# Chunk-selecting attention with a softplus MLP on one core: transposes by DMA, halved first preparation, a new load order

## The chip, the cores and the metric

The kernel runs on one core of one Trainium2 chip. The metric is the device time of one execution in microseconds (us), as a median over several executions. Names used below: PE is TensorE (PEld its weight loads), DVE is VectorE, ACT is ScalarE, POOL is GpSimd, SP is SyncE, which here only issues DMAs.

## The reference

```python
# q, k, v: (4 batches, 8 heads, 768, 64); moe_w_in: (512, 2048); moe_w_out: (2048, 512); all float32
k_min, k_max = min and max of k over each chunk of 32 keys          # 24 chunks
ub = sum_d(max(q * k_min, q * k_max))                               # upper bound for each query and chunk
top_chunks = the 6 chunks of highest ub (only chunks up to the query's own)
attn = softmax(q @ k.T / 8, over the keys of those chunks, causal)
x = (attn @ v) with the heads side by side                          # (3072, 512)
h = x @ w_in
g = max(h, 0) + log1p(exp(-abs(h)))                                 # softplus
out = g @ w_out                                                     # (3072, 512)
```

## The kernel before

The work goes in 12 blocks of 256 queries. A block has four parts: *preparation* (turn k and q so that the head dimension lies on the partitions, chunk minima and maxima `kx`, bounds `ub`, the mask), *scores* (`s_ps`, `exp` into `pt`), *AV* (`o_ps`, normalised into `o_sb`, turned into `x`), and the *MLP* (`hp`, softplus, `y`). Preparation, attention and MLP of different blocks are interleaved by slots: a slot is one `yield` of the score loop. Block 3i has 8 slots, block 3i+1 has 16, block 3i+2 has 24.

Every transpose is a TensorE matmul with the identity, followed by a copy out of PSUM, the memory that matmuls write to:

```python
def prep_block(n):                                     # cut
    kT = ps_t.tile([128, NP, QB], BF16, name="kT", tag="t")
    for t in range(NT):
        for p in range(NP):
            nc.tensor.transpose(kT[:, p, t * 128:(t + 1) * 128], k_sb[:, t, 2 * p:2 * p + 2, :], ident)
    nc.scalar.copy(kt, kT)
    nc.vector.tensor_reduce(kx[:, :, 0], kT4, axis=AX.X, op=ALU.max)    # kT4 is a view of kt
    nc.vector.tensor_reduce(kx[:, :, 1], kT4, axis=AX.X, op=ALU.min)
    ...
    yield
    # then qT in the same way, the bounds, and mT, the transposed mask
def ot_step(n, p, o_sb):
    oT = ps_t.tile([128, QB], BF16, name="oT", tag="t")
    for u in range(NT):
        nc.tensor.transpose(oT[:, u * 128:(u + 1) * 128], o_sb[:, u], ident)
    nc.vector.tensor_copy(X[n][:, p], oT)
```

Blocks 0 to 2 are loaded as float32 by SP (half of block 0 by ACT's queue) and cast by ACT; later blocks and the weights are loaded by POOL with a cast in the DMA. The order is: blocks 0, 1, 2, then w_in, then w_out.

The order of the instructions on an engine is either that of the source ("manual") or that of the compiler's list scheduler. POOL and SP are manual throughout. PE, ACT and DVE are manual in block 0 alone:

```python
ctx.enter_context(tc.manual_schedule(engines={ET.Pool, ET.SP}))
...
with tc.manual_schedule(engines={ET.Activation, ET.DVE, ET.PE}):
    ...
    run_block(0, 0.0)
... # cut: block 2's loads
run_block(1, 0.8)
for n in range(2, NB):
    run_block(n, 1.0 if n > 2 else 0.8)
```

The softmax here doesn't subtract the row's maximum and nothing guards it: scores larger than these inputs give would overflow.

## Time and profile before

| | before |
|---|---|
| median of the first three runs | 316.74 us (316.65 to 318.0) |
| profiled span | 314.1 us |
| PE, ACT, DVE busy | 86%, 71%, 56% |
| first `exp` of block 2 | 55.7 us |
| from there to the end | 258.4 us |

The last two rows are read from ACT's timeline, by counting its `exp` instructions (8, 16, 24 for a block). They split the span into a start, in which PE starves, and a later stage.

The first lines of the page of the kernel before. The strings of digits cut the span into 40 slices; a digit is the busy share of a slice in tenths, PEclk is the clock granted to TensorE in tenths.

```profile
span 314.1 us, 6878 instructions
...
PE 270.5 (86%) x2748; PEld 198.6 (63%) x2784; DVE 174.4 (56%) x550; ACT 224.2 (71%) x379; POOL 99.0 (32%) x172
...
PE   1335879989899799899999799899999999999983
...
PEclk9999959999999999999999999999999999999999
DMA  9999899993933906904913905907900000001101
```

PE is thin for five slices (40 us), then near full. Next, groups of the same kernel: line, engine, operation, tiles, shapes, count, then busy time in us and mean ns of one, then the idle time of the engine just before them and what ended it.

```profile
L305 DVE COPY x<-oT 128x256 bf16<-128x256 bf16 x48 | 13.9, 289 | 25.1 <-PE oT L304 24.8
...
L304 PE MATMUL oT<-ident,o_sb 128*128 128x128 bf16 x96 | 13.7, 225 | 4.3 <-DVE o_sb L293 4.3
...
L236 PE MATMUL mT<-ident,mraw_114 128*64 128x128 bf16 x48 | 4.7, 253 | 3.4 <-DVE mraw_114 L230 3.2
```

These are the round trips that the change wants to remove: PE waits for DVE, turns, and DVE copies back.

### The profile page before, as it was taken

The page shows a single profiled execution, that of the slowest core. Times are in us where ns is not written, and L with a number is a line of the kernel's source. Part 1 is how long each engine was busy: PE and PEld are TensorE (multiplying, and loading weights), DVE is VectorE, ACT ScalarE, POOL GpSimd, SP SyncE. Part 2 cuts the span into 40 slices and gives each one's busy share as a digit, 9 for nine tenths or more (in the row PEclk, how much of TensorE's full clock was granted, in tenths as well). Part 3 has the DMA queues.
Part 4 walks back from the last instruction along what each step waited for, and adds up shares of the span by engine and source line. Part 5 has one row for each costly group of instructions (what it writes and reads, how often), then busy time and mean ns, then how long its engine had stood idle before and what let it go on. Part 6 is the DMA issues. An engine that isn't in the chain of part 4 may idle for free.

```text
span 314.1 us, 6878 instructions
## 1 busy us (share of the span) xinstructions
PE 270.5 (86%) x2748; PEld 198.6 (63%) x2784; DVE 174.4 (56%) x550; ACT 224.2 (71%) x379; POOL 99.0 (32%) x172
## 2 busy tenths in 40 slices
PE   1335879989899799899999799899999999999983
PEld 0223657667658667677658577677568777776651
DVE  5818582592965964935946946836748732112100
ACT  4578789968837858788628868888539769983550
POOL 4024375622723613514624414424421211111000
PEclk9999959999999999999999999999999999999999
DMA  9999899993933906904913905907900000001101
GB/s 165 200 216 216 147 158 189 92 71 45 80 73 52 83 11 60 101 2 57 90 59 53 83 35 33 102 3 76 94 33 35 3 33 35 2 33 35 67 17 52
DMA packets 82208, 23.51 MB, mean 75 GB/s; under 512 B 75520, under 2 KB 78080, under 8 KB 82176
## 3 DMA queue, kind: packets, MB, share of 16 engines
q0 software_dynamic: 59424, 11.28, 43.9%
q1 hardware_dynamic: 19632, 11.01, 14.3%
q10 hardware_dynamic: 3120, 0.79, 1.4%
q8 instruction: 21, 0.34, 0.4%
q14 instruction: 11, 0.09, 0.1%
HBM read 27.26 MB, written 6.29 MB: 107 GB/s over the span
## 4 chain that ended last, share of the span: by engine, by line
PE 57%; DVE 26%; ACT 12%; issue 2%; DMA 1%; ACTq 0%; DVEq 0%
PE y L335 21%; PE hp L322 17%; PE o_ps L285 5%; PE s_ps L263 4%; DVE kx L181 4%; ACT kt L179 4%; DVE kx L182 4%; PE s_ps L265 3%; PE mT L236 3%; ACT pt L267 2%; DVE qneg L204 2%; ACT e_sb L324 2%; DVE qpos L203 2%; DVE qt L200 2%; DMA xf<-in_k_dram 1%
## 5 line engine op out<-in xcount | busy, mean ns | idle before, releaser
L267 ACT ACTIVATE pt<-s_ps 128x512 bf16<-128x512 f32 (+1 forms) x192 | 103.9, 556 | 36.7 <-PE s_ps L265 29.9
L322 PE MATMUL hp<-x,w_in_sb 128*128 128x256 bf16 x768 | 103.5, 273 | 3.2 <-ACT e_sb L324 1.8
L271 POOL TENSOR_SCALAR_AFFINE_SELECT pt<-pt 128x256 bf16<-128x256 bf16 x96 | 40.9, 426 | 185.5 <-ACT pt L267 185.1
L335 PE MATMUL y<-w_out_sb,g 128*128 128x512 bf16 x348 | 90.7, 379 | 3.6 <-DVE y_sb L340 1.7
L322 PEld LDWEIGHTS <-w_in_sb 128*128 128x128 bf16 x768 | 71.4, 98 | 12.9 <-issue 4.1
L324 ACT ACTIVATE e_sb<-hp 128x512 f32<-128x512 f32 x96 | 58.4, 611 | 27.7 <-PE hp L322 27.4
L335 PEld LDWEIGHTS <-g 128*128 128x128 bf16 x384 | 34.2, 97 | 28.6 <-issue 2.8
L326 ACT ACTIVATE g<-e_sb 128x1024 bf16<-128x1024 f32 x48 | 51.8, 1078 | 0.3
L285 PEld LDWEIGHTS <-pt 128*128 128x128 bf16 x672 | 32.9, 99 | 11.1 <-issue 4.3
L340 DVE COPY y_sb<-y 128x512 f32<-128x512 f32 x24 | 16.5, 687 | 39.7 <-PE y L335 39.5
L291 DVE RECIPROCAL rec<-o_ps 128x4 f32<-128x4 f32 x48 | 8.5, 177 | 38.1 <-PE o_ps L285 37.9
L305 DVE COPY x<-oT 128x256 bf16<-128x256 bf16 x48 | 13.9, 289 | 25.1 <-PE oT L304 24.8
L285 PE MATMUL o_ps<-v_106,pt 128*128 128x65 bf16 x336 | 20.7, 199 | 2.2 <-DVE o_sb L293 1.9
L181 DVE TENSOR_REDUCE kx<-kt 128x32 bf16<-128x1024 bf16 x12 | 14.6, 1219 | 13.0 <-ACT kt L179 13.0
L293 DVE TENSOR_TENSOR o_sb<-o_ps,rec 128x256 bf16<-128x256 f32 x48 | 20.2, 422 | 1.3
L285 PE MATMUL o_ps<-v_107,pt 128*128 128x65 bf16 x336 | 18.4, 193 | 1.7 <-DVE o_sb L293 1.5
L304 PE MATMUL oT<-ident,o_sb 128*128 128x128 bf16 x96 | 13.7, 225 | 4.3 <-DVE o_sb L293 4.3
L114 POOL DMA_DIRECT2D k_sb<-in_k_dram x18 | 16.1, 892 | 0.8 <-issue 0.5
L114 POOL DMA_DIRECT2D q_sb<-in_q_dram x18 | 16.2, 902 | 0.4 <-issue 0.3
L175 PE MATMUL kT<-ident,k_sb 128*128 128x128 bf16 x96 | 8.8, 241 | 8.1 <-ACT k_sb L103 7.6
L263 PE MATMUL s_ps<-qt,kb_110 128*128 128x256 bf16 x48 | 14.0, 293 | 1.6 <-ACT pt L267 0.9
L263 PE MATMUL s_ps<-qa,ka_108 96*128 96x256 bf16 x48 | 14.2, 296 | 0.8 <-DVE qa L241 0.8
(111 smaller groups left out, 365.2 us busy)
## 6 DMA issues: line engine op xcount, KB each, us to landing
out_dram<-y_sb SPq DMA_DIRECT2D x24, 256.0 KB, 2.0
k_sb<-in_k_dram POOLq DMA_DIRECT2D x18, 128.0 KB, 3.8
q_sb<-in_q_dram POOLq DMA_DIRECT2D x18, 128.0 KB, 4.3
w_in_sb<-in_moe_w_in_dram POOLq DMA_DIRECT2D x8, 256.0 KB, 6.9
w_out_sb<-in_moe_w_out_dram POOLq DMA_DIRECT2D x4, 512.0 KB, 9.5
v_107<-in_v_dram POOLq DMA_DIRECT2D x12, 128.0 KB, 5.3
xf<-in_k_dram SPq DMA_DIRECT2D x5, 256.0 KB, 5.1
xf<-in_q_dram SPq DMA_DIRECT2D x5, 256.0 KB, 5.8
```

The costliest lines, as they stand in the source:

```text
L114: nc.gpsimd.dma_start(out=xb[:, t], in_=rows(nm, n, t))
L181: nc.vector.tensor_reduce(kx[:, :, 0], kT4, axis=AX.X, op=ALU.max)
L263: nc.tensor.matmul(s_ps[:, 0:QB], kk[0:nr, p, j * 128:(j + 1) * 128], qq[0:nr, p, :], start=True, stop=True)
L267: nc.scalar.activation(pt[:, h, j:j + 2].rearrange("k j c -> k (j c)")[:, 0:w], s_ps[:, 0:w], ACT.Exp, scale=scale)
L271: nc.gpsimd.affine_select(out=diag, in_=diag, compare_op=ALU.is_ge, fill=0.0, base=0, channel_multiplier=-1, pattern=[[0, 2], [1, 128]])
L285: nc.tensor.matmul(o_ps[:, u, h], pt[:, h, j, c0:c0 + 128], V[b % 2][:, j, 2 * p + h, :], start=(j == 0), stop=(j == t0 + u))
L293: nc.vector.tensor_tensor(o_sb, o_ps[:, :, :, 0:D], rec.to_broadcast([128, NT, 2, D]), op=ALU.mult)
L322: nc.tensor.matmul(hp[:, fi], w_in_sb[:, dt, ft * 128:(ft + 1) * 128], X[n][:, dt], start=(dt == 0), stop=(dt == KDM - 1))
L324: nc.scalar.activation(e_sb[:, f2 * 2:f2 * 2 + 2], hp, ACT.Exp)
L326: nc.scalar.activation(g[:, f4 * 4:(f4 + 1) * 4], e_sb, ACT.Ln, bias=1.0)
L335: nc.tensor.matmul(y, g[:, f, u * 128:(u + 1) * 128], w_out_sb[:, f, :], start=(f == 0), stop=(f == KFF - 1))
L340: nc.vector.tensor_copy(y_sb, y)
```

## The change

From block 2 on, k, q and the mask are transposed by DMA, and in every block the output; these DMAs (*turns*) are issued on the SP queue. The chunk extremes `kx` of these blocks are now called `kxf`. The first two blocks are prepared by halves of the head pairs. The loads come as blocks 0 and 1, w_in, w_out, block 2. PSUM is dealt out anew, and some pools have more buffers. The core of the diff, with cuts:

```diff
-    pt_pool = ctx.enter_context(tc.tile_pool(name="pt", bufs=3))
+    pt_pool = ctx.enter_context(tc.tile_pool(name="pt", bufs=5))
-    ps_o = ctx.enter_context(tc.tile_pool(name="ps_o", bufs=1, space=PS))
-    ps_t = ctx.enter_context(tc.tile_pool(name="ps_t", bufs=2, space=PS))
+    ps_o = ctx.enter_context(tc.tile_pool(name="ps_o", bufs=2, space=PS))
+    ps_t = ctx.enter_context(tc.tile_pool(name="ps_t", bufs=1, space=PS))
...
+    def turn_dma(nm, n, pool):
+        x_sb = loaded.pop((nm, n))
+        xt = pool.tile([128, NT, NP, 128], BF16, name=nm + "t")
+        nc.sync.dma_start_transpose(out=xt.rearrange("d t p s -> d (t p) s"),
+                                    in_=x_sb.rearrange("s t h d -> s (t h d)"))
+        turned[nm, n] = xt
...
     def prep_block(n):                                 # from block 2 on
-        (kT by TensorE, copy by ACT)
+        kt = turned.pop(("k", n))
+        kx = prep.tile([128, 2, NT, NP, CH // 8], BF16, name="kxf")
         for t in range(NT):
+            kc = kt[:, t].rearrange("d p (c e) -> d p c e", e=CH)
+            nc.vector.tensor_reduce(kx[:, 0, t], kc, axis=AX.X, op=ALU.max)
+            nc.vector.tensor_reduce(kx[:, 1, t], kc, axis=AX.X, op=ALU.min)
+            yield
...
+        nc.sync.dma_start_transpose(out=mt.rearrange("c t g s -> c (t g) s"),
+                                    in_=mraw.rearrange("s t p h c -> s (t p h c)"))
...
     def ot_step(n, g, o_sb):                           # two head pairs at a time
+        nc.sync.dma_start_transpose(
+            out=X[n][:, g].rearrange("d u p s -> d (u p) s"),
+            in_=o_sb.rearrange("s u p h d -> s (u p h d)"))
+        if g == 1:
+            ready[n] = clock[0] + 4                    # hp waits 4 slots more
...
+        base = PER * (n - 1) - PER // 2 + 2            # kxf stands in slot base; 17 for block 2
+        at(base - (4 if n > 2 else 1), turns)          # the turn of k
+        at(base - (3 if n > 2 else 1), turns)          # the turn of q
...
+        at(1, hold(xfs["q", 1][0:1, 1, 7, 0:1]))       # POOL waits for block 1's q
+        loads.append(load_w_in())
+        loads.append(load_cast("v", 1))
+        loads.append(load_w_out())
+        block_loads(2)
```

## The prediction

> **What bounds the kernel now.** Span 314.1 us; engine shares: PE 86%, ACT 71%, DVE 56%. Until about 60 us PE starves (slice row 1, 3, 3, 5, 8 tenths at first), waiting for loads and the preparation chains of blocks 0 to 2; w_in's last piece is issued at 36.2 us and lands about 7 us later; w_out's last is issued at 43.4 and first used at 58.6. After that PE is the limit. Start-to-start distances of matmuls in dense stretches of the timeline: 109 ns for 256 columns, 215 for 512, about 30 for the 65-column AV matmuls, 56 for a 128x128 transpose. All matmuls at these distances are about 249 us of PE work: hp 84, y 83, scores 36, AV 20, transposes 21, bounds 5. By 60 us only 22 us is done; the other 227 take 254 us, so about 27 us of the later stage is waiting. The groups table places some: oT 4.3 us for o_sb, mT 5.1, AV 3.9; the distances before oT and mT matmuls from 60 to 300 us add to 18 us for 8.6 us of work. The chain of waits has DVE 26% and ACT 12%, mostly preparation.
>
> **Removed.** PE loses 344 of 384 transposes (the instruction order shows 688 fewer PE rows, matmul plus weight load): 344 x 56 ns = 19 us, about 17 of it after 60 us. DVE loses 48 oT copies (13.9 us) and 9 qT copies (6.1); ACT loses kt and qt copies of 1.0 us and casts. Round trips for oT and mT vanish; two AV banks, five pt and x buffers loosen the rest.
>
> **Added.** Five transposing DMAs a block on the SP queue, 0.9 MB. None is in this trace. The Trainium skill ("DMA: Bandwidth & Descriptors", section "Latency and other measured facts") states 261 GB/s effective for one kind of transposing DMA; with the 2.0 us that a store takes here from issue to landing, 256 KB would take an estimated 3 us. The schedule gives them 3 to 5 slots of about 1.2 us: hidden, with small stalls.
>
> **Startup.** Blocks 0 and 1 are prepared faster (first scores near 15 us instead of 17; block 1 near 30 instead of 35), and w_in lands 10 us earlier. But block 2's k and q come after w_out, at an estimated 46 to 50 us by the read rates of the trace (about 210 GB/s for float loads, 340 to 400 for the casting weight loads); then transposes, preparation and mask follow. Block 2's scores start near 60 us, as before.
>
> **Sum.** From block 2: 213 us of PE work instead of 227; waiting 27 -> about 17 us, as h-only stretches stay ACT-bound. 60 + 213 + 17 = 290, perhaps 2 less from startup: span 288, time **290 us**, 8-in-10 range **277 to 303**. Chances: faster 0.89, same 0.06, slower 0.05.
>
> **What would show it.** About 2,400 PE matmuls; ACT total about 215 us; transposing DMAs landing in 3 to 5 us; few waits of DVE for kt and qt; w_in landed by 33 us; block 2's scores near 60 us.
>
> **What would make it wrong.** Transposing DMAs of 8 us or more, or queued on SP behind waiting ones: kx and hp would then wait in each block (20 us or more too slow). Block 2's loads landing at 40 us instead of 48: 8 us faster. ACT becoming the limit.

## The result, and the profile after

The changed kernel takes **338.19 us** (336.81 to 338.91, 4 runs) against 317.24 (316.65 to 318.0, 4 runs) for the kernel before: 1.065 times as long, 95% interval 1.0607 to 1.0701. Ratios here are the mean time of one kernel's fast runs over that of the other's fast runs of the same rounds, so they are not quite the ratio of the medians quoted. The prediction was 290 us and faster; the kernel is slower by over 2%.

The same lines of the page of the changed kernel:

```profile
span 337.0 us, 6388 instructions
...
PE 261.4 (78%) x2411; PEld 185.2 (55%) x2440; DVE 168.5 (50%) x615; ACT 197.2 (59%) x350; POOL 115.7 (34%) x191
...
PE   1234579428978879589899699299898799999994
...
PEclk9999999856997999969999979789999799999999
DMA  9929999996995992946966949937946211011101
```

The transposes are gone from PE (2,411 matmuls), and PE is busy for 9 us less, but the span is 23 us longer. PE has a hole near 60 to 80 us and dips all through the later stage, and most dips come with a lower granted clock. The first `exp` of block 2 is at 79.7 us instead of 55.7; from there to the end it is 257.3 us instead of 258.4. So the start lost 24 us, and the later stage gained 1 us in place of the gain of about 28 us that the prediction counted on (258.4 to 213 + 17 = 230).

Who waited for whom in the changed kernel (in us: total, times, longest); the waits for transposing DMAs are new:

```profile
DVE kxf L289 <- DMA kt<-k_sb: 30.1, 9, 7.8
...
PE y L415 <- DVE y_sb L420: 17.2, 7, 6.0
...
PE hp L402 <- DMA x<-o_sb: 11.1, 3, 8.1
...
DVE qa L279 <- DMA mt<-mraw_115: 8.3, 5, 2.7
DVE qa L279 <- DMA mt<-mraw_114: 7.7, 4, 3.3
```

The wait of `y` has a small counterpart in the kernel before:

```profile
PE y L335 <- DVE y_sb L340: 1.7, 3, 0.8
```

The median time from issue to landing of the transposing DMAs:

```profile
x<-o_sb SPq DMA_TRANSPOSE x24, 3.2
...
kt<-k_sb SPq DMA_TRANSPOSE x10, 4.7
qt<-q_sb SPq DMA_TRANSPOSE x10, 5.1
mt<-mraw_114 SPq DMA_TRANSPOSE x5, 2.5
```

That is what the prediction expected in the middle (3 to 5 us). One place of the later stage shows how it hurts all the same. First DVE's timeline around the preparation of block 9 (start, duration, engine, line, operation, in brackets the idle time before it):

```profile
203.77 0.42 DVE L373 TENSOR_TENSOR o_sb<-o_ps,rec 128x256 bf16<-128x256 f32 x1
212.00 0.69 DVE L289 TENSOR_REDUCE kxf<-kt 128x16 bf16<-128x512 bf16 x1 [7.81 <-DMA kt<-k_sb]
...
216.85 0.68 DVE L420 COPY y_sb<-y 128x512 f32<-128x512 f32 x1
```

The SP queue at the same time:

```profile
204.22 1.19 SPq L381 DMA_TRANSPOSE x<-o_sb  x1
205.51 1.25 SPq L166 DMA_TRANSPOSE kt<-k_sb  x1
206.93 1.53 SPq L166 DMA_TRANSPOSE qt<-q_sb  x1
```

And PE:

```profile
217.58 1.86 PE L415 MATMUL y<-w_out_sb,g 128*128 128x512 bf16 x4 [6.02 <-DVE y_sb L420]
```

DVE stands at `kxf` from 204.2 us, 1.3 us *before* the DMA that `kxf` needs is even issued. The k that it turns had been loaded by 186.6 us. The copy `y_sb`, which has nothing to do with block 9, stands behind `kxf`; PE cannot start the next `y` and idles for 6.0 us. When it starts again, a 512-column matmul takes about 430 ns from start to start instead of 215: the clock record shows half rate from 214.8 us for 6.8 us. The Trainium skill ("TensorE: Matmul & The Clock Gate", section "What's actually happening") says that after an idle window of about 3.4 us the array is given half of the clock pulses until it has been busy for such a window. This trace agrees in the lengths: its six half-rate stretches before the end last 3.4, 6.8 or 17.1 us, 40.9 us in all, and the kernel before had one of 6.8 us. It agrees less in what comes before them: PE's idle gaps just ahead of the six are 8.1, 2.9, 4.5, 2.8, 6.0 and 1.9 us, so half of them are shorter than the window.

### The profile page after: what moved, and what is told of

Same layout as the page of the kernel before. It is cut to its first block, busy times and chain, and to the rows that moved or that the text cites. A ratio compares the mean times of both kernels' runs of the same rounds, so it can differ in the third digit from the quotient of the medians.

```text
span 337.0 us, 6388 instructions
## 1 busy us (share of the span) xinstructions
PE 261.4 (78%) x2411; PEld 185.2 (55%) x2440; DVE 168.5 (50%) x615; ACT 197.2 (59%) x350; POOL 115.7 (34%) x191
## 3 DMA queue, kind: packets, MB, share of 16 engines
q0 software_dynamic: 67168, 12.33, 48.9%
## 4 chain that ended last, share of the span: by engine, by line
PE 43%; DVE 23%; DMA 20%; ACT 4%; SPq 3%; POOL 3%; issue 2%; ACTq 0%
PE y L415 19%; PE hp L402 13%; DMA kt<-k_sb 10%; PE o_ps L363 4%; PE s_ps L338 3%; DVE y_sb L420 3%; DMA q_sb<-in_q_dram 3%; DMA two<-in_k_dram 3%; DVE kxf L290 3%; DVE kxf L289 3%; PE s_ps L340 2%; DMA x<-o_sb 2%; DVE bd_112 L191 2%; DMA qt<-q_sb 2%; DVE qpos L298 1%
## 5 line engine op out<-in xcount | busy, mean ns | idle before, releaser
L402 PE MATMUL hp<-x,w_in_sb 128*128 128x256 bf16 x768 | 107.1, 283 | 11.9 <-DMA x<-o_sb 11.1
L415 PE MATMUL y<-w_out_sb,g 128*128 128x512 bf16 x355 | 96.9, 395 | 19.1 <-DVE y_sb L420 17.2
L402 PEld LDWEIGHTS <-w_in_sb 128*128 128x128 bf16 x768 | 74.6, 101 | 23.8 <-issue 11.8
L404 ACT ACTIVATE e_sb<-hp 128x512 f32<-128x512 f32 x96 | 57.8, 605 | 31.7 <-PE hp L402 31.6
L289 DVE TENSOR_REDUCE kxf<-kt 128x16 bf16<-128x512 bf16 x20 | 13.6, 680 | 30.2 <-DMA kt<-k_sb 30.1
L373 DVE TENSOR_TENSOR o_sb<-o_ps,rec 128x256 bf16<-128x256 f32 x48 | 20.2, 422 | 1.4 <-DVE rec L369 0.3
L113 POOL DMA_DIRECT2D k_sb<-in_k_dram x20 | 17.8, 894 | 8.4 <-DMA kt<-k_sb 4.8
L363 PE MATMUL o_ps<-v_106,pt 128*128 128x65 bf16 x336 | 20.2, 202 | 0.1
L113 POOL DMA_DIRECT2D q_sb<-in_q_dram x20 | 18.0, 904 | 1.9 <-DMA qt<-q_sb 1.3
L363 PE MATMUL o_ps<-v_107,pt 128*128 128x65 bf16 x336 | 16.3, 195 | 0.8 <-DVE o_sb L373 0.8
L203 DVE TENSOR_TENSOR ub_sb<-ub,cmask 128x192 f32<-128x192 f32 x20 | 7.0, 352 | 16.7 <-PE ub L202 16.7
L338 PE MATMUL s_ps<-qt,kb_110 128*128 128x256 bf16 x48 | 14.9, 311 | 0.4 <-ACT pt L342 0.3
L279 DVE COPY qa<-mt 32x512 bf16<-32x512 bf16 x20 | 6.7, 333 | 16.4 <-DMA mt<-mraw_115 8.3
L338 PE MATMUL s_ps<-qt,kb_111 128*128 128x256 bf16 x48 | 13.5, 281 | 0.0
```

Source lines behind the costliest of these rows:

```text
L113: nc.gpsimd.dma_start(out=xb[:, t], in_=rows(nm, n, t))
L289: nc.vector.tensor_reduce(kx[:, 0, t], kc, axis=AX.X, op=ALU.max)
L338: nc.tensor.matmul(s_ps[:, 0:QB], kk[0:nr, p, j * 128:(j + 1) * 128], qq[0:nr, :, p, :], start=True, stop=True)
L363: nc.tensor.matmul(o_ps[:, u, h], pt[:, h, j, c0:c0 + 128], V[b % 2][:, j, 2 * p + h, :], start=(j == 0), stop=(j == t0 + u))
L373: nc.vector.tensor_tensor(o_sb[:, :, p % 2], o_ps[:, :, :, 0:D], rec.to_broadcast([128, NT, 2, D]), op=ALU.mult)
L402: nc.tensor.matmul(hp[:, fi], w_in_sb[:, dt, ft * 128:(ft + 1) * 128], X[n][:, dt // 2, :, dt % 2, :], start=(dt == 0), stop=(dt == KDM - 1))
```

## The experiments

Two theories at first. **Start**: block 2's loads come last, block 2 starts 24 us late, and that runs through to the end. **Turns**: the transposing DMAs of k and q hold up DVE in every block. A third came up later. The kernel before was timed at 316.3 to 317.5 us. All kernels gave the reference's result.

### One part undone or moved: a_order, a_lead, a_pekq, a_allpe

**a_order**: block 2 ahead of w_out.

```diff
-        loads.append(load_w_out())
         block_loads(2)
+        loads.append(load_w_out())
```

> The changed kernel with block 2's loads put ahead of w_out. Theory 1 (the load order made block 2 start 24 us late and this delay was carried to the end): block 2's k and q land near 47 us instead of 58, its first exp moves from 79.7 to about 66-69 us, and the time falls by about 8 to 12 us, to 326-330 us. Theory 2 (the loss comes from the transposing DMAs of every block, and startup is absorbed because PE has work in store anyway): block 2 starts earlier but the time falls by less than 4 us.

Measured: 339.31 us, as slow as the change. Block 2's k and q did land at 46.9 and 49.7 us, but block 2 began at 78.3. The time from issue to landing of the turn of q in this run (minimum, median, maximum):

```profile
DMA to landing us min/median/max: 3.9/6.0/13.9
```

The 13.9 us is the turn of block 2's q, in flight from 49.8 to 63.7 us, beside w_out's pieces (issued from 48.9 us on, landed from 57.9 to 67.7). So the delay only moved from the load to the turn. This fits what the Trainium skill says ("DMA: Bandwidth & Descriptors", section "Issuing engines are not separate DMA queues"): DMAs of all issuing engines share the same 16 DMA engines and interleave. The run does not decide between the theories.

**a_lead**: the turns 4 slots earlier.

```diff
-        at(base - (4 if n > 2 else 1), turns)
-        at(base - (3 if n > 2 else 1), turns)
+        at(base - (8 if n > 3 else 4 if n > 2 else 1), turns)
+        at(base - (7 if n > 3 else 3 if n > 2 else 1), turns)
```

> The changed kernel with the k and q transposing DMAs issued 4 slots earlier from block 4 on. Theory 2 (DVE waits 30 us in nine places for kt because the turn is issued behind stores on the SP queue and lands late): the wait of DVE for kt falls from 30 us to below 15 us and the time falls by 8 us or more. Theory 1 (startup is the loss): the time changes by under 3 us.

Measured: 322.64 us, 15.5 us less than the change, with the start as it was (block 2 at 79.5 us). The wait of DVE for kt fell to 15.1 us, but did not vanish. So lead alone regains most of the loss here.

**a_pekq**: k and q turned by TensorE again, at the same places.

```diff
-        nc.sync.dma_start_transpose(out=xt.rearrange("d t p s -> d (t p) s"), ...)
+        xT = ps_t.tile([128, NT, NP, 128], BF16, name="xTf", tag="t")
+        for t in range(NT):
+            for p in range(NP):
+                nc.tensor.transpose(xT[:, t, p], x_sb[:, t, 2 * p:2 * p + 2, :], ident)
+        (nc.scalar.copy if nm == "k" else nc.vector.tensor_copy)(xt, xT)
```

> The changed kernel with k and q turned by TensorE again in every block (mask and output stay with the DMA). Theory 2: no wait for kt or qt DMAs, time falls by 8 us or more although PE gets 160 transposes (9 us) back; block 2's first exp also 5 to 8 us earlier as no DMA stands between load and use. Theory 1: about 3 to 8 us gained at block 2's start and about as much lost to the transposes, time within 4 us of 338.

Measured: 314.61 us. These 160 transposes, given *back* to PE, save 23.6 us.

**a_allpe**: the mask and the output by TensorE as well.

> The changed kernel with all transposes from block 2 on by TensorE: what stays of the change is the new first preparation, the load order and the buffers. Theory 1: still slow, 325 us or more, since the startup is kept. Theory 2: back near the kernel before, 310 to 320 us.

Measured: 318.68 us. So the 21.4 us between the change (338.19, timed before) and the 316.8 of the kernel before split into: +1.9 for everything except the DMA transposes (a_allpe), -4.1 for the mask and the output by DMA (a_allpe to a_pekq), +23.6 for k and q by DMA (a_pekq to the change). The turns theory stands; what the start does is not yet told.

### Waiting, or load on the DMA engines? a_pekq_dummy

k and q come from TensorE, but their DMAs are issued all the same, into tiles that nobody reads (`pt` with 4 buffers instead of 5 makes the room).

```diff
         (a_pekq's transposes and copies)
+        nc.sync.dma_start_transpose(out=idle[nm].rearrange("d t p s -> d (t p) s"),
+                                    in_=x_sb.rearrange("s t h d -> s (t h d)"))
```

> As the run with k and q turned by TensorE (314.6 us), but the transposing DMAs of k and q are still issued too, into tiles that nothing reads (pt with four buffers instead of five, to make room for them). So their queue time and their share of the DMA engines stay, only the wait for their result is gone. Wait theory (DVE stands behind kt in program order, that is the cost): 313-318 us. Rival (the transposes slow down the loads, the output and mask transposes and the SP queue): 322 us or more, most of the way back to 338.

Measured: 318.7 us, 4.1 more than a_pekq. Queue time, contention and the missing `pt` buffer are thus worth about 4 us together, and waiting for the result about 19.5 of the 23.6 us. The 4 us lie in the start: block 2 begins at 78.7 us instead of a_pekq's 74.8, and the later stages take 238.2 and 238.4 us.

### The start, and more lead: a_early, a_pekq_early, a_lead_early, a_pekq_early2, a_pekqm_early2, a_lead_early2

**a_early** loads k and q of block 2 beside the pieces of w_in:

```diff
-        at(1, hold(...)); loads.append(iter((1,))); loads.append(load_w_in())
+        at(0, hold(...))
+        loads.append(zip(load_w_in(), chain(load_cast("k", 2), load_cast("q", 2))))
         loads.append(load_cast("v", 1)); loads.append(load_w_out())
-        block_loads(2)
+        loads.append(load_cast("v", 2))
```

> The changed kernel with k and q of block 2 loaded beside the pieces of w_in (two loads a slot) and nothing else changed. So block 2's k and q are there about 20 us earlier and their transposing DMAs no longer meet the w_out loads only by chance. Start theory (block 2's start is late because its loads come last, and the delay runs through to the end): block 2's first exp moves from 79.7 to 60-66 us and the time falls by 10 us or more, to 322-328. Rival (the later stage is limited by late kt turns whatever the start, and work left over is caught up in it): time falls by less than 4 us, as in the run with block 2 ahead of w_out.

Measured: 333.96 us, 4.2 less; block 2 at 74.6 us, 5 us earlier. The later stage stays at 257.3 us, so what the start gained was not lost again. A turn of k took up to 8.7 us: it was again in flight beside w_out. Both parts of the expectation were too far apart; the truth lay between.

**a_pekq_early** is this with a_pekq's turns.

> The same earlier loads, and k and q turned by TensorE. If start and transposing DMAs are two separate losses, both gains add: block 2's first exp near 60-63 us and the time 298-304 us, clearly under the 316.8 of the kernel before. If the start only shifts waiting, it stays at 310-315.

Measured: 309.9 us, with block 2 at 71.6: 4.7 us better than a_pekq. The gains add, but are small: the time lies between the two ranges expected (298 to 304 and 310 to 315).

**a_lead_early** is a_early with the turns 4 slots earlier in every block (8 slots ahead from block 4 on, 6 and 5 in blocks 3 and 2).

> All transposes by DMA as in the change, with the earlier loads and the k and q turns issued 4 slots earlier in every block. If the change failed only by its schedule (lead too short, block 2's loads last) this beats the kernel before: 300-308 us. If transposing DMAs cost more than lead (contention with the casting loads, waits for mask and output), it stays at 312 us or more and 8 us or more behind the run with TensorE for k and q.

Measured: 321.56 us, 11.7 behind a_pekq_early. More lead, and still 18.3 us of waiting for kt.

**a_pekq_early2** moves block 2's preparation from slots 17 to 23 to slots 10 to 21 (`base = 10`).

> The run of 309.9 us (early loads, k and q by TensorE) with block 2's preparation moved from slots 17-23 to slots 10-21, as its data is there. If the late slots of that preparation are the rest of the start's loss, block 2's first exp moves from 71.6 to about 59-62 us and the time falls to 299-304 us. If the start is set by something else (DVE work of blocks 1 and 2 together), under 3 us gain.

Measured: 314.38 us, 4.5 *slower* than a_pekq_early, a miss, although block 2 began at 68.9. DVE's wait for the mask's DMA rose from 20.2 to 25.2 us, with one wait of 6.6 us.

**a_pekqm_early2** has the mask by TensorE too (five more lines, as in the kernel before).

> The same with the mask transposed by TensorE too, so that only the output goes by DMA. DVE waits 18-20 us for the mask's DMA in the run with k and q by TensorE. If that wait costs time, 3 us faster than the run with the mask by DMA; if it is idle time that costs nothing, within 1.5 us, or slower by the 4 us of PE work of 80 transposes.

Measured: 309.26 us, 5.1 better than with the mask by DMA. Most of it is in the start: block 2 at 64.3 us instead of 68.9.

**a_lead_early2** keeps all DMA transposes, with early loads, lead, and block 2's preparation in slots 12 to 23.

> All transposes by DMA, as in the change, with early loads, k and q turned 8 slots ahead and block 2's preparation in slots 12-23. If lead and order were all that failed, 304-310 us. If turns near the weight loads stay slow (8 us and more landing), 314 us or more.

Measured: 313.16 us, as the median of three executions (312.46 to 314.83; the fourth, 319.02, was slow). That is above the range of the first theory and just short of that of the second. Still, the schedule alone brings the change to just below the kernel before (0.989 times).

### Parts of the change on the old start: b_xdma, b_xdma_buf, a_allpe_buf

**b_xdma**: the kernel before, with only the output by DMA.

```diff
-        oT = ps_t.tile([128, QB], BF16, name="oT", tag="t")
-        for u in range(NT):
-            nc.tensor.transpose(oT[:, u * 128:(u + 1) * 128], o_sb[:, u], ident)
-        nc.vector.tensor_copy(X[n][:, p], oT)
+        nc.sync.dma_start_transpose(out=X[n][:, p].rearrange("d (u s) -> d u s", s=128),
+                                    in_=o_sb.rearrange("s u h d -> s (u h d)"))
         done[n] += 1
+        if done[n] == NP:
+            ready[n] = clock[0] + 4
```

> The kernel before with only the output transposes moved to DMA (48 of them, one for each head pair, hp held 4 slots longer). Taking 96 transposes (5.4 us of PE) and 48 copies (13.9 us of DVE) away and the 11 us of waits before oT: if those round trips did cost PE time, 305-311 us; if PE just finds other waits, within 3 us of 316.8.

Measured: 306.54 us, 0.967 times the kernel before (95% interval 0.9641 to 0.9693). This part of the prediction's idea was sound.

**b_xdma_buf** adds the change's PSUM split (two AV banks, one for transposes).

> The kernel before with the output by DMA (306.5 us), PSUM as in the change: two AV banks and one bank for the transposes, in place of one and two. Two AV banks take away the 3.5 us that PE waits for o_sb; one bank for kT, qT, ub, mT makes the preparation serial. Expected within 3 us of 306.5; if the later stage's gain in the run with k and q by TensorE comes from the AV banks, 300-304.

Measured: 305.51 us, 1 us better.

**a_allpe_buf**: a_allpe with the old buffers.

> The changed kernel with all later transposes by TensorE (318.7 us) and, in addition, the buffers of the kernel before (o_ps 1 and ps_t 2, pt 3, st 3, x 4). If the new start costs time (block 2's first exp 15 us late) and the deeper buffers hide it, this goes to 325 us or more. If start and buffers both matter little, it stays within 3 us of 318.7.

Measured: 316.33 us, 2.4 *less* than with the new ones. The buffers hide no loss.

### Why lead in the source is not enough: b_xkq, b_xkq_buf, a_dve, b_xkq_dve

**b_xkq**: b_xdma, and from block 3 on k and q by DMA, issued 7 and 6 slots ahead.

```diff
+    def turns(n):
+        for nm, pool in (("k", prep), ("q", qt_pool)):
+            x_sb = loaded.pop((nm, n))
+            xt = pool.tile([128, NP, QB], BF16, name=nm + "t")
+            turned[nm, n] = xt
+            for t in range(NT):
+                nc.sync.dma_start_transpose(out=xt[:, :, t * 128:(t + 1) * 128],
+                                            in_=x_sb[:, t].rearrange("s h d -> s (h d)"))
+            yield
...
+            at(base - 7, tn)
+            at(base - 6, tn)
```

> The kernel before with the output by DMA (306.5 us) and, from block 3 on, k and q by DMA too, issued 7 and 6 slots ahead of use. If lead is what decides, the 144 transposes less (8 us of PE work) show: 299-304 us. If turns of k and q cost DVE waits even so: 306 us or more.

Measured: 331.31 us, 25 us *more* than b_xdma, in spite of old start, long lead and less PE work. **b_xkq_buf**, the same with the PSUM split, is hardly different:

> The output, k and q by DMA with lead, and the PSUM of the change; with no kT and qT in it one bank is enough for the later blocks. If both gains add: 298-302 us. If the PSUM is worth nothing: as the run without it.

Measured: 329.78 us. So here neither lead in the source nor banks bring the gain. The built program shows another cause. Here is DVE's order around the same `kxf` of block 9 as above, in the changed kernel as the scheduler left it (the numbers count instructions on DVE; this is not a profile and has no time in it):

```
281 L369 Reciprocal rec<-o_ps 128x4
282 L280 TensorCopy qt<-mt 32x4x128
283 L373 TensorTensor o_sb<-o_ps,rec 128x2x128
284 L289 TensorReduce kxf<-kt 128x16
285 L290 TensorReduce kxf<-kt 128x16
286 L369 Reciprocal rec<-o_ps 128x4
...
```

and with DVE kept in the order of the source:

```
281 L280 TensorCopy qt<-mt 32x4x128
282 L279 TensorCopy qa<-mt 32x4x128
283 L280 TensorCopy qt<-mt 32x4x128
284 L369 Reciprocal rec<-o_ps 128x4
285 L373 TensorTensor o_sb<-o_ps,rec 128x2x128
286 L420 TensorCopy y_sb<-y 128x512
287 L289 TensorReduce kxf<-kt 128x16
```

In the source a normalisation (`rec`, `o_sb`) and a `y_sb` copy stand ahead of `kxf`; the scheduler moved `kxf` before them. Counting `rec` and `y_sb` ahead of each block's first `kxf` in both orders: from block 6 to block 11 it is always one `y_sb` fewer, in four of the six also one `rec` fewer; in blocks 2, 3 and 5 it is one `rec` more. In b_xkq it is worse: two to three `rec` fewer from block 4 on, for instance 11 in place of 14 in block 5. And with a_lead's 8 slots the trace has `kxf` three `rec` ahead of the source order in blocks 8 and 11, two in block 5 (13 in place of 15) and one in blocks 6, 7, 9 and 10: lead in the source was partly spent by the reordering. This is the third theory, **hoist**. Two runs test it; each sets DVE to source order from block 1 on and changes nothing else.

```diff
-    run_block(1, 0.8)
-    for n in range(2, NB): ...
+    with tc.manual_schedule(engines={ET.DVE}):
+        run_block(1, 0.8)
+        for n in range(2, NB): ...
```

**a_dve**, on the changed kernel:

> The changed kernel with VectorE kept in source order from block 1 on (PE and ACT still ordered by the compiler's scheduler), no other edit. In the built program the scheduler puts kxf ahead of one rec or y_sb copy that the source has before it in seven of ten blocks, and in the trace DVE stands at kxf within 4 us of the turn's issue, sometimes before it. Hoist theory (the cost is that everything behind kxf on DVE waits for the DMA): PE's wait for y_sb falls from 17 us to under 7, the wait of DVE for kt falls below 15 us, and the time falls by 8 us or more, to 330 or less. Latency theory (the 3 to 8 us that a turn takes are simply longer than the 4 slots): the time changes by under 4 us.

("Seven of ten" there is a miscount; it is the six of ten blocks told above.) Measured: 315.86 us, 22 us less than the change, with not one transpose moved. Its waits:

```profile
DVE kxf L289 <- DMA kt<-k_sb: 18.6, 5, 10.3
...
PE y L415 <- DVE y_sb L420: 1.4, 3, 0.8
```

PE's wait for `y_sb` went from 17.2 to 1.4 us. DVE still waits 18.6 us for kt, over the bound that the expectation set (15), but 10.3 of it is one wait, in block 2 at the start. Its wait for the mask's DMA fell too, from 16.0 to 3.4 us, so source order helped more than one reader. The later stage takes 236.0 us, 21.3 less; how much of that is the shorter half-rate time after block 2's start (14 us instead of 26) was not taken apart.

**b_xkq_dve**, on b_xkq:

> The run with output, k and q by DMA on the old start (331.3 us) with VectorE in source order from block 1 on. There the scheduler put kx two to three rec's earlier than the source does, which eats the 7 slots of lead. Hoist theory: the wait of DVE for kt falls from 40.7 us to under 10 us and the time to 299-306 us, so that the transposes taken from PE pay. Latency or contention theory: 320 us or more.

Measured: **296.84 us** (296.58 to 298.97), 0.9377 times the kernel before (95% interval 0.934 to 0.9414), the fastest of all. DVE's wait for kt, first in b_xkq:

```profile
DVE kx L194 <- DMA kt<-k_sb: 40.7, 9, 8.0
...
PE mT L250 <- DVE rec L305: 17.0, 4, 7.4
```

and then in b_xkq_dve:

```profile
PE mT L250 <- DVE rec L305: 1.7, 1, 1.7
...
DVE kx L194 <- DMA kt<-k_sb: 2.3, 1, 2.3
```

The page of b_xkq_dve:

```profile
span 294.8 us, 6598 instructions
...
PE 257.5 (87%) x2544; PEld 185.4 (63%) x2544; DVE 150.4 (51%) x493; ACT 214.9 (73%) x370; POOL 98.2 (33%) x172
...
PE   1245663987999999999999999999999999999984
...
PEclk9999999999999999999999999999999999999998
```

PE is full from a fourth of the span on, and the clock stays up.

The traces show the lead that was left. Take the moment at which DVE was free for a block's first `kxf` or `kx` (its start less the idle time before it), and subtract the start of the last issue of that block's turn of k. The median over blocks 3 to 11 is 2.2 us in the changed kernel and 6.2 us in a_dve, 0.7 us in b_xkq and 8.6 us in b_xkq_dve. The same turns landed after 4.3 and 3.7 us, and after 5.1 and 5.3 us. So in the second pair the DMA was as slow as before; it is the place of its reader that changed.

## Why the prediction was wrong

- **"hidden, with small stalls" is the step that failed**, and it took most of the gain with it. The landing time was right in the middle (predicted 3 to 5 us, medians 2.4 to 5.1), but the lead of "3 to 5 slots" was read from the source, and DVE did not run in the order of the source. `kxf` was moved ahead of other work and made it wait for the DMA. The Trainium skill says of ACT and DVE that they are "strict FIFO" ("TensorE: Matmul & The Clock Gate", section "Architectural detail: the array is 16× 32×32, not 1× 128×128"), and the timeline agrees: `y_sb` stood behind `kxf` and the preparation after it until 216.85 us, and PE with it. Source order on DVE alone takes 22 us off the change and 34 us off b_xkq. The built order could have been listed before the prediction was made; I counted PE rows with it and did not look where `kxf` stood.
- **"waiting 27 -> about 17 us"** fell with it. The later stage took 257.3 us in place of 230. With DVE in source order it takes 236.0 (a_dve) and 235.3 us (b_xkq_dve). The remaining 5 to 6 us are not taken apart.
- **"Block 2's scores start near 60 us, as before"** was wrong by 20 us. The loads landed at 57.8 (k) and 59.5 us (q) instead of 46 to 50; w_in, ahead of them on the same queue, was there at 38.0 instead of 33. The turns then took 8.3 and 9.6 us instead of 3, beside the casting loads of block 3; preparation and mask took the last 10 us. a_dve and b_xkq_dve have later stages equal to 1 us and differ by 18.5 us in block 2's start and by 19.0 us in time, so such a start can cost its full length. a_early, a_pekq and a_pekqm_early2 moved it to 74.6, 74.8 and 64.3; no single run restores it within the change.
- **The removed work was right**: 344 transposes less (2,440 weight loads recorded instead of 2,784), and the round trips for oT were worth more than their PE time: b_xdma gains 10 us. ACT's total came out at 197 us instead of 215; it was never the limit.
- **The chance of "slower", 0.05, was too low.** Of the dangers named (8 us and more, or queueing on SP), both came true at block 2's start: its turns took 8.3 and 9.6 us, and block 1's first output turn, ready at 59.6 us, was issued behind q's turn at 63.2, so that PE waited 8.1 us for it. In the later stage the longest turn of k took 6.5 us. There each turn of k was issued 0.1 us after another DMA on SP, but so it was in a_dve; what I missed is that a wait of 5 us does harm where it stands in front of other work. Nor did I count that gaps of PE are followed by stretches of half clock (40.9 us in all).

The predicted range was not out of reach: with the old start, the mask still on TensorE and DVE in source order the idea gives 296.84.

Left open: the kernel before, and b_xdma, were not run with DVE in source order, so what source order gives by itself, without DMA turns, is not known; b_xkq to b_xkq_dve shows it only where they are present. A kept trace narrows this: in b_xdma, which has no turns of k and q, the scheduler leaves `kx` of blocks 3 to 11 behind exactly as many `rec` and `y_sb` as b_xkq_dve's source order does. Nor was source order run together with a_lead's longer lead. Why a_allpe, with block 2 15 us late, ends so close to the kernel before is not explained: its later stage is 13 us shorter (245.0 us, 316.1 less 71.1), and a_allpe_buf shows that the buffers are not the reason. Why block 2's preparation in earlier slots made a_pekq_early2 slower was only seen beside a longer wait for the mask, not shown to come from it. What duration the scheduler assumes for a transposing DMA was not looked at.

## What to carry to other kernels

When work moves from an engine to a DMA, look in the built order for where the first reader of its result stands on its own in-order engine, and what stands behind it: lead given in the source is no lead if a scheduler moves the reader forward. Give the DMA route first to results with slack (here the output, 10 us gained by itself), and to those on a preparation chain only with the reader's place fixed (306.5 to 296.8 us with it, to 331.3 without). Keep transposing DMAs out of the time in which large casting loads run: here they took up to 13.9 us beside them, against medians of 2.4 to 5.1.

## What the Trainium skill lacked or had wrong

- "DMA: Bandwidth & Descriptors": it gives a bandwidth for transposing DMAs (261 GB/s) and no time from issue to landing between SBUF tiles. Here a 128x1024 bf16 turn took 3.1 us at best, 4.7 to 5.1 in the median, 8.3 to 9.6 beside casting loads and up to 13.9 beside w_out; a 128x512 one 2.4 us at best. The estimate from it, 3 us, was the best case.
- The same page: for the issuing queue it has only sequencer cycles of "previous generations", beside those of a later chip, and no time for a turn of this size. Here it was 1.19 to 1.25 us on SP for each where SP was not held up, so five a block fill 6 us of the queue.
- "TensorE: Matmul & The Clock Gate": the lengths of the half-rate stretches (3.4, 6.8 and 17.1 us) agree with its window of about 3.4 us. That a whole idle window must come first (section "What's actually happening") is not what the trace shows: three of the six followed gaps of 1.9 to 2.9 us, with PE at work before and after.
- I found no page that says that, beside the hardware's own order, the order in which a compiler's scheduler leaves an engine's instructions has to be read: here it was worth 22 us (a_dve) and 34 us (b_xkq_dve).
